# The last output tile: half of it copied out of PSUM by two engines and stored by rows on two queues

## The chip, the cores and the metric

The kernel runs on one core of one Trainium2 chip. The core has a matrix engine (PE in the profile), VectorE (DVE), ScalarE (ACT), GpSimd (POOL) and SyncE (SP), which work side by side and meet through semaphores, and 16 DMA engines that move data between the chip's main memory and the core. DMAs are issued here from two queues: SP's (SPq) and ScalarE's (ACTq). The metric is the device time of one execution in microseconds, from the start of the program to its end.

## The reference

The input `x` has 2048 rows of 512 bf16 numbers. It is normalised by rows, and two branches read the normalised rows: a linear attention with 32 heads and softmax feature maps, and a two-layer network of width 1792 with the mish activation. Both are added to `x`:

```python
x = A_x
xn = _layernorm(x, axis=-1)
return x + _A_ref(xn, A_wqkv, A_w_phi, A_wo) + _B_ref(xn, B_w1, B_b1, B_w2)
```

The attention ends in `o @ wo`, a product over 512 columns, and the network in `act @ w2`, a product over 1792. So one row of the output is the sum of three things: 14 products of 128 columns with `w2`, 4 with `wo`, and the row of `x` itself.

## The kernel before, in words

The 2048 rows are cut into 16 tiles of 128 rows. `x` lies in SBUF in one tile `x_sb` of 16 row tiles, is loaded at the start, and is overwritten by the output at the end. The weights lie in SBUF as well; `w2_sb` is loaded at about 20 us in three DMAs (line 646).

The order of all the work is written out by hand, as the names in `PLAN`; a loop at the end of the function calls `step` for each name, and each engine gets its instructions in that order. Nothing is moved by a scheduler. What the framework adds are the semaphores: each instruction waits for the writers and readers of the memory that it touches. The DMAs take their completion semaphores from a ring of eight, in the order in which they stand in the program, and a DMA waits for the DMA that had the same semaphore eight places before.

In the last stage, each output tile `t` goes through these names:

- `second_t_0` and `second_t_1` (`second_layer`, line 524): 14 matmuls of 128 rows and 512 columns from `acts` and `w2_sb` into one PSUM bank, `po`.
- `project_t` (`project_out`, line 533): 4 matmuls with `wo` into the same bank. Their input `ob` is a tile that a DMA on SP's queue transposed before (`turn_out`, line 512).
- `residual_t` (line 541): one VectorE instruction that adds `po` to the tile of `x_sb` and writes the tile back.
- `store_t` (line 545): a DMA of 128 rows of 1024 bytes to the output, on SP's queue.

The last tile, 15, is treated apart: `halves` gives it two halves of 256 columns, each with a PSUM bank of its own. So it has 28 + 8 matmuls of 256 columns, two additions on VectorE, and two stores of 128 rows of 512 bytes: that of the first half is issued on ScalarE's queue, that of the second on SP's. The end of the plan reads

```
project_12 second_15_0 residual_12 store_12 store_11 project_13 second_15_1 residual_13 store_13
project_14 project_15 residual_14 store_14 residual_15 store_15
```

After the last store the program waits for the semaphores of the DMAs that are still under way, and closes with two barriers over all engines.

Of the kernel before, what the change touches and what calls it, by code (L numbers as in the profile page):

```python
# [13 lines left out]
ALU = mybir.AluOpType  # L14
# [71 lines left out]
def kernel(  # L86
# [12 lines left out]
    nc = tc.nc  # L99
    P = 128  # L100
    S, D, NH, DH, F = 2048, 512, 32, 16, 1792
    NG = 4
    TPG = 4
    NT = NG * TPG
# [6 lines left out]
    o_v = out.flatten_outer_dims().rearrange("(t p) d -> p t d", p=P)  # L111
# [18 lines left out]
    def bank(name, dtype=FP32):  # L130
        return ps.tile([P, 512], dtype, name=name, tag="mm")

    x_sb = persist.tile([P, NT, D], BF16, name="x_sb")
# [15 lines left out]
    ident = consts.tile([P, P], BF16, name="ident")  # L149
# [46 lines left out]
    def spread(t):  # L196
        nc.vector.bn_stats(statistics(t)[0][:, t % TPG, :], x_sb[:, t, :])  # L197

    def total(t):
        negated.add(t)  # L200
        mv = statistics(t)[1][:, t % TPG, :]
        nc.scalar.activation(junk[:], x_sb[:, t, :], ACT.Identity, scale=-1.0 / D, accum_out=mv[:, 0:1])

    def scatter(t):
        mv = statistics(t)[1][:, t % TPG, :]
        nc.scalar.activation(
            junk[:], x_sb[:, t, :], ACT.Square, bias=mv[:, 0:1], accum_out=mv[:, 1:2]
        )

    def gather(t, n):  # L210
        stats, mv, _, _ = ln_of[t // TPG]
        for i in range(t % TPG, t % TPG + n):
            nc.vector.bn_aggr(mv[:, i, :], stats[:, i, :])

    def deviate(t, n):
        _, mv, rstd, _ = ln_of[t // TPG]
        i = slice(t % TPG, t % TPG + n)
        nc.scalar.activation(rstd[:, i], mv[:, i, 1], ACT.Sqrt, bias=eps[:],  # L218
            scale=1.0 / D if t in negated else 1.0)

    def invert(t, n):
        rstd = ln_of[t // TPG][2][:, t % TPG : t % TPG + n]
        nc.vector.reciprocal(rstd, rstd)  # L223
# [30 lines left out]
    def turn_pe(t):  # L254
        ptr = bank("ptr", BF16)
        for kt in range(KT):
            nc.tensor.transpose(  # L257
                ptr[:, kt * P : (kt + 1) * P], xn_of[0][:, t, kt * P : (kt + 1) * P], ident[:]
            )
        return ptr[:].rearrange("p (k c) -> p k c", k=KT)  # L260
# [255 lines left out]
    def halves(t):  # L516
        return (slice(0, 256), slice(256, 512)) if t == NT - 1 else (slice(0, 512),)

    def second_layer(t, f0, f1):
        if f0 == 0:  # L520
            po_of[t] = [bank("po") for c in halves(t)]
        for po, c in zip(po_of[t], halves(t)):
            for f in range(f0, f1):
                nc.tensor.matmul(  # L524
                    po[:, c], lhsT=acts[:, f, t * P : (t + 1) * P], rhs=w2_sb[:, f, c],
                    start=(f == 0), stop=False,
                )

    def project_out(t):
        h = t // 2  # L530
        for po, c in zip(po_of[t], halves(t)):
            for j in range(4):
                nc.tensor.matmul(  # L533
                    po[:, c], lhsT=oT_of[h][:, 2 + t % 2, j * P : (j + 1) * P], rhs=wo_sb[:, j, c],
                    start=False, stop=(j == 3),
                )

    def residual(t):
        for po, c in zip(po_of.pop(t), halves(t)):
            y = x_sb[:, t, c]  # L540
            nc.vector.tensor_tensor(out=y, in0=po[:, c], in1=y, op=ALU.add)  # L541

    def store(t):
        for n, c in enumerate(halves(t)):
            (nc.scalar if c.stop == 256 else nc.sync).dma_start(o_v[:, t, c], x_sb[:, t, c])


    with nc.allow_non_contiguous_dma(reason="tiny w_phi load"):
# [18 lines left out]
    for sign in (1, -1):  # L567
        nc.gpsimd.affine_select(
            out=block[:], in_=block[:], pattern=[[-16 * sign, 8], [0, 16]],
# [13 lines left out]
    def keep_warm():  # L583
        nc.tensor.matmul(warm[:], lhsT=one((P, P)), rhs=one((P, 512)), start=True, stop=True)
# [8 lines left out]
    def step(name):  # L593
# [5 lines left out]
        if kind == "warm":  # L599
            keep_warm()  # L600
        elif kind == "spread":
            spread(*n)
        elif kind == "block":
            nc.gpsimd.tensor_tensor(
                out=Wbd[:].rearrange("p j (h e) -> p j h e", h=8),
                in0=block[:, None, :, :].to_broadcast([P, 4, 8, 16]),
                in1=wsrc[:, :, None, :].to_broadcast([P, 4, 8, 16]),
                op=ALU.mult,
            )
        elif kind == "total":  # L610
            total(*n)
        elif kind == "scatter":
            scatter(*n)
        elif kind == "mean":
            gather(n[0], 1)
        elif kind == "deviate":
            deviate(*n)
        elif kind == "invert":
            invert(*n)
        elif kind == "flip":  # L620
            held[key] = turn_pe(*n)
        elif kind == "flip=":
            copies[alt](xnT[:, n[0], :, :], held.pop(key))  # L623
        elif kind == "foldk":
            held[key] = fold(held["wT"], *n)
        elif kind == "foldk=":
            copies[alt](wkp[:, n[0], :], held.pop(key)[:])  # L627
        elif kind == "first":
            i, kt = n
            held["logits", 0, i] = project(wkp, i, held.get(("logits", 0, i)), range(kt, kt + 1))  # L630
        elif kind == "bias":
            held[key] = bank("pb", BF16)
            nc.tensor.transpose(held[key][:, 0:FT], b1b[:], ident[0:FT, 0:FT])
        elif kind == "bias=":
            nc.vector.tensor_copy(b1f[:], held.pop(key)[:, 0:FT])
        elif kind == "gather":
            gather(TPG * n[0], TPG)
        elif kind == "root":
            root_inverse(*n)
        elif kind == "apply":  # L640
            apply(*n, sides[alt])
        elif kind == "turned":
            turn_dma(*n)
        elif kind == "w2":
            for f in (slice(0, 5), slice(5, 10), slice(10, 14)):
                nc.sync.dma_start(w2_sb[:, f, :], w2_v[:, f, :])
        elif kind == "wo":
            nc.sync.dma_start(wo_sb, wo_v[:, :, :])
        elif kind == "wq":
            held["wT"] = load_turned(0)  # L650
        elif kind == "fold":
            held[key] = fold(held["wT"], *n)
        elif kind == "fold=":
            copies[alt](wqp[:, n[0], :], held.pop(key)[:])
        elif kind == "value":
            held[key] = project(wv, *n)
        elif kind == "value=":
            value_copy(*n, held.pop(key), copies[alt])
        elif kind == "logits":
            held[key] = project(wkp if n[0] < NG else wqp, n[0] % NG * TPG + n[1])  # L660
        elif kind == "logits=" and n[0] in MERGED:
            signed_copy(*n, held[key], 1, sides[2 - 2 * alt])
        elif kind == "minus=":
            signed_copy(*n, held.pop(("logits", *n)), -1, sides[2 - 2 * alt])
        elif kind == "shift":
            shifted(n[0], slice(2 * n[1], 2 * n[1] + 2))
        elif kind == "logits=":
            logits_copy(*n, held.pop(key), copies[alt])
        elif kind == "plane":
            extremes(*n[0:2], *(slice(2 * q, 2 * q + 2) for q in n[2:]))  # L670
        elif kind == "exp":
            exponential(*n)
        elif kind == "sums":
            sums(*n, sides[alt])
        elif kind == "normal":
            normalise(*n)
        elif kind == "add":
            accumulate(*n)
        elif kind == "masks":
            masks()  # L680
        elif kind == "kv":
            mask_kv()
            kvp.close()
            later.append(ctx.enter_context(tc.tile_pool(name="pq", bufs=1, space=PSUM)))
        elif kind == "unit":
            held[key] = hidden(*n)
        elif kind == "unit=":
            activate(*n, held.pop(key))
        elif kind == "weigh":
            weigh(*n)  # L690
        elif kind == "turn":
            turn(*n)
        elif kind == "attend":
            attend(*n)
        elif kind == "divide":
            divide(*n)
        elif kind == "out":
            turn_out(*n)
        elif kind == "second":
            second_layer(n[0], 7 * n[1], 7 * n[1] + 7)  # L700
        elif kind == "project":
            project_out(*n)
        elif kind == "residual":
            residual(*n)
        elif kind == "store":
            store(*n)
# [33 lines left out]
```

## Time and profile before

| | |
|---|---|
| median of 3 runs | 174.26 us (174.21 to 174.62) |
| profiled execution | 174.22 us |
| its span, first to last instruction | 172.5 us |
| PE busy | 168.5 us, 98% of the span |
| VectorE busy | 150.6 us, 87% |
| ScalarE busy | 113.0 us, 66% |
| granted PE clock | 0.999 |

The profiled execution took 174.22 us, of which 172.5 us lie between its first and its last instruction; the 1.72 us that remain lie around the span. Times within the trace count from the start of the span. A row of the timeline gives the start and the length in microseconds, the engine, the line and the operation, what it writes and reads with the shape, how many instructions of a kind follow each other, and in brackets how long the engine had been idle before and what ended that. `SPq` and `ACTq` rows are the issuing of DMAs. A row of groups gives the total busy time and the mean duration of one in ns.

### The profile page before, as it was taken

How to read it: one execution, taken by the hardware profiler on the slowest of the kernel's cores; microseconds unless marked ns; L12 is line 12 of the kernel's file. 1: busy time of each engine (PE TensorE's matmuls, PEld its weight loads, DVE VectorE, ACT ScalarE, POOL GpSimd, SP SyncE). 2: the span in 40 equal slices, each digit the busy share in tenths (PEclk: the TensorE clock that was granted, in tenths of full speed). 3: DMA queues.
4: the chain of work that ended last, by engine and by line, in shares of the span. 5: the costliest groups of instructions: out<-in, count | busy, mean ns of one | idle time of the engine just before them, and what ended most of it. 6: DMA issues, size and time to landing. Idle time of an engine off the chain costs nothing.

```text
span 172.5 us, 2832 instructions
## 1 busy us (share of the span) xinstructions
PE 168.5 (98%) x1038; PEld 82.6 (48%) x1038; DVE 150.6 (87%) x265; ACT 113.0 (66%) x169; POOL 49.5 (29%) x91
## 2 busy tenths in 40 slices
PE   8999999999999999999999999999999999999993
PEld 2444444444544644455454444544544554445571
DVE  2967998999999999999999999999999899994633
ACT  4949999999999799999999998821710400400000
POOL 6003047100480005685007403341480420320000
PEclk9999999999999999999999999999999999999999
DMA  6999992647900000000000095217456556676752
GB/s 154 264 397 347 130 331 89 128 117 143 104 0 0 4 0 0 2 0 4 0 0 0 0 131 117 61 37 163 47 121 138 130 130 93 143 164 152 124 143 71
DMA packets 45226, 18.03 MB, mean 105 GB/s; under 512 B 37148, under 2 KB 45212, under 8 KB 45212
## 3 DMA queue, kind: packets, MB, share of 16 engines
q1 hardware_dynamic: 44496, 17.26, 44.5%
q10 hardware_dynamic: 716, 0.59, 1.1%
q8 instruction: 8, 0.13, 0.3%
q14 instruction: 6, 0.05, 0.1%
HBM read 6.84 MB, written 2.10 MB: 52 GB/s over the span
## 4 chain that ended last, share of the span: by engine, by line
PE 94%; DVE 2%; DMA 1%; ACT 1%; issue 0%; DVEq 0%
PE ph L289 28%; PE po L524 28%; PE pproj L274 24%; PE po L533 8%; PE pnd L488 2%; PE pkv L451 2%; DMA x_sb<-in_A_x_dram 1%; DVE stats L197 1%; PE pfold L174 1%; DVE x_sb L541 1%; PE ptr L257 1%; DVE xn L249 0%; ACT wkv L627 0%; ACT rstd L218 0%; DVE rstd L223 0%
## 5 line engine op out<-in xcount | busy, mean ns | idle before, releaser
L524 PE MATMUL po<-w_sb,acts 128*128 128x512 bf16 (+1 forms) x238 | 51.9, 366 | 0.0
L289 PE MATMUL ph<-xnT,w_sb 128*128 128x512 bf16 x224 | 50.9, 379 | 0.0
L377 ACT ACTIVATE e<-e 128x1024 bf16<-128x1024 bf16 x28 | 28.3, 1056 | 25.1 <-DVE e L347 25.0
L391 POOL TENSOR_TENSOR t<-e 128x512 f32<-128x512 bf16 x13 | 16.6, 1274 | 78.2 <-ACT e L377 78.1
L299 ACT ACTIVATE acts<-ph,b1f 128x512 bf16<-128x512 f32 x56 | 35.4, 706 | 1.2 <-PE ph L289 1.1
L289 PEld LDWEIGHTS <-w_sb 128*128 128x128 bf16 x224 | 21.5, 98 | 25.2 <-issue 0.4
L524 PEld LDWEIGHTS <-acts 128*128 128x128 bf16 x238 | 22.5, 98 | 22.9
L274 PE MATMUL pproj<-wkv,xnT 128*128 128x512 bf16 x128 | 29.4, 379 | 0.0
L274 PEld LDWEIGHTS <-xnT 128*128 128x128 bf16 x192 | 18.0, 98 | 20.1 <-ACT xnT L623 0.3
L387 DVE TENSOR_REDUCE sums<-e 128x64 f32<-128x1024 bf16 x15 | 17.9, 1212 | 1.0 <-ACT e L377 0.8
L391 POOL TENSOR_TENSOR t<-t 128x256 f32<-128x256 f32 (+1 forms) x28 | 16.1, 576 | 2.2
L533 PE MATMUL po<-wqk,ob 128*128 128x512 bf16 (+1 forms) x68 | 16.3, 366 | 0.0
L274 PE MATMUL pproj<-wqk,xnT 128*128 128x512 bf16 x64 | 15.3, 379 | 0.0
L541 DVE TENSOR_TENSOR x_sb<-po,x_sb 128x512 bf16<-128x512 f32 (+1 forms) x17 | 10.9, 650 | 4.1 <-PE po L533 4.1
L197 DVE BATCH_NORM_STATS2 stats<-x_sb 128x6 f32<-128x512 bf16 x15 | 9.4, 679 | 4.1 <-DMA x_sb<-in_A_x_dram 4.1
L504 DVE TENSOR_TENSOR ob<-pnd,r 128x512 bf16<-128x512 f32 x16 | 11.1, 691 | 0.5
L438 DVE TENSOR_TENSOR e<-e,r 128x2048 bf16<-128x2048 bf16 x8 | 9.9, 1231 | 0.3
L326 ACT CAST e<-pproj 128x512 bf16<-128x512 f32 x12 | 7.1, 605 | 4.4 <-PE pproj L274 3.9
L533 PEld LDWEIGHTS <-ob 128*128 128x128 bf16 x68 | 6.4, 98 | 6.0
L503 DVE RECIPROCAL r<-pnd 128x32 f32<-128x32 f32 x16 | 5.6, 351 | 4.0 <-PE pnd L488 3.8
L309 ACT CAST p<-pproj 128x512 bf16<-128x512 f32 x14 | 7.8, 597 | 1.6 <-PE pproj L274 1.6
L488 PEld LDWEIGHTS <-qT 128*128 128x128 bf16 x128 | 6.1, 97 | 3.9 <-issue 0.9
(80 smaller groups left out, 184.6 us busy)
## 6 DMA issues: line engine op xcount, KB each, us to landing
out_dram<-x_sb SPq DMA_DIRECT2D x15, 128.0 KB, 1.9
w_sb<-in_B_w_dram SPq DMA_DIRECT2D x2, 896.0 KB, 8.4
x_sb<-in_A_x_dram SPq DMA_DIRECT2D x3, 512.0 KB, 10.2
w_sb<-in_B_w_dram SPq DMA_DIRECT2D x2, 640.0 KB, 5.5
wkv<-in_A_wqkv_dram SPq DMA_DIRECT2D x1, 512.0 KB, 5.1
w_sb<-in_B_w_dram SPq DMA_DIRECT2D x1, 512.0 KB, 7.0
wqk<-in_A_wo_dram SPq DMA_DIRECT2D x1, 512.0 KB, 4.2
x_sb<-in_A_x_dram ACTq DMA_DIRECT2D x1, 384.0 KB, 3.2
```

What stands on the lines that cost most here:

```text
L197: nc.vector.bn_stats(statistics(t)[0][:, t % TPG, :], x_sb[:, t, :])
L274: nc.tensor.matmul(pp, lhsT=xnT[:, t, kt, :], rhs=w[:, kt, :], start=(kt == 0), stop=(kt == KT - 1),)
L289: nc.tensor.matmul(ph[:], lhsT=w1_sb[:, kt, f * P : (f + 1) * P], rhs=xnT[:, g * TPG : (g + 1) * TPG, kt, :], start=(kt == 0), stop=(kt == ...
L299: nc.scalar.activation(acts[:, f, g * 512 : (g + 1) * 512], ph[:], ACT.Mish, bias=b1f[:, f : f + 1])
L377: nc.scalar.activation(v, v, ACT.Exp)
L387: nc.vector.reduce_sum(out, part, axis=AX.X)
L391: nc.gpsimd.tensor_tensor(out=to[:], in0=part[:, :, 0:n], in1=part[:, :, n : 2 * n], op=ALU.add)
L438: nc.vector.tensor_tensor(out=vv, in0=vv, in1=r2[:, :, None, :].to_broadcast([P, 128, 8, 2]), op=ALU.mult)
L504: nc.vector.tensor_tensor(out=o_t.rearrange("p (u v g d) -> p u v g d", u=2, v=4, g=4), in0=nd[:, :, :, 0:64].rearrange("p u v (g d) -> p ...
L524: nc.tensor.matmul(po[:, c], lhsT=acts[:, f, t * P : (t + 1) * P], rhs=w2_sb[:, f, c], start=(f == 0), stop=False,)
L533: nc.tensor.matmul(po[:, c], lhsT=oT_of[h][:, 2 + t % 2, j * P : (j + 1) * P], rhs=wo_sb[:, j, c], start=False, stop=(j == 3),)
L541: nc.vector.tensor_tensor(out=y, in0=po[:, c], in1=y, op=ALU.add)
```

## The change

Three places are edited. In the last tile's second half (columns 256 to 511), an added matmul of the identity with the last 128 columns of `x` adds these columns into PSUM, right after the first matmul of that half. Its end is then written out in two parts: ScalarE copies columns 384 to 511, in which `x` is already contained, and VectorE adds columns 256 to 383 as before. The store of that half is cut by rows: rows 0 to 63 on ScalarE's queue, rows 64 to 127 on SP's. The store of the first half, which was on ScalarE's queue, is now issued on SP's. And `w2` is loaded in two DMAs of seven blocks in place of three of five, five and four, so that the number of DMAs in the program is as before.

```diff
@@ second_layer
                     start=(f == 0), stop=False,
                 )
+                if f == 0 and turned_in(t, c):
+                    nc.tensor.matmul(
+                        po[:, 384:512], lhsT=ident[:], rhs=x_sb[:, t, 384:512],
+                        start=False, stop=False,
+                    )
@@
+    def turned_in(t, c):
+        return t == NT - 1 and c.stop == D
+
     def residual(t):
         for po, c in zip(po_of.pop(t), halves(t)):
             y = x_sb[:, t, c]
-            nc.vector.tensor_tensor(out=y, in0=po[:, c], in1=y, op=ALU.add)
+            if turned_in(t, c):
+                nc.scalar.copy(out=y[:, 128:256], in_=po[:, 384:512])
+                nc.vector.tensor_tensor(
+                    out=y[:, 0:128], in0=po[:, 256:384], in1=y[:, 0:128], op=ALU.add
+                )
+            else:
+                nc.vector.tensor_tensor(out=y, in0=po[:, c], in1=y, op=ALU.add)
 
     def store(t):
         for n, c in enumerate(halves(t)):
-            (nc.scalar if c.stop == 256 else nc.sync).dma_start(o_v[:, t, c], x_sb[:, t, c])
+            if turned_in(t, c):
+                for q, rows in ((nc.scalar, slice(0, 64)), (nc.sync, slice(64, 128))):
+                    q.dma_start(o_v[rows, t, c], x_sb[rows, t, c])
+            else:
+                nc.sync.dma_start(o_v[:, t, c], x_sb[:, t, c])
@@ step
         elif kind == "w2":
-            for f in (slice(0, 5), slice(5, 10), slice(10, 14)):
+            for f in (slice(0, 7), slice(7, 14)):
                 nc.sync.dma_start(w2_sb[:, f, :], w2_v[:, f, :])
```

## The prediction

> **What bounds the kernel now.** I read the page's busy shares first, then the chain that ended last, then the timeline of the last four microseconds, engine by engine.
>
> ```profile
> span 172.5 us, 2832 instructions
> PE 168.5 (98%) x1038; PEld 82.6 (48%) x1038; DVE 150.6 (87%) x265; ACT 113.0 (66%) x169; POOL 49.5 (29%) x91
> ```
>
> PE is busy all the time; what follows its last matmul is uncovered. The chain, asked from 160 us on, shows both:
>
> ```profile
> 165.45 0.86 PE po L533 x4
> 166.31 1.53 PE po L524 x14
> 167.84 0.88 PE po L533 x4
> 168.72 0.02 issue
> 168.74 1.02 DVE x_sb L541 x2
> 169.76 0.33 DVEq L735
> ```
>
> PE's pieces follow each other without a gap, so whatever is added on PE there moves the end by its full length. From 168.74 the chain is VectorE's: tile 14's addition, then the two halves of tile 15. The timeline in short windows gives the pieces (a row that names several instructions runs from the first one's start to the last one's end):
>
> ```profile
> 168.74 0.69 DVE L541 TENSOR_TENSOR x_sb<-po,x_sb 128x512 bf16<-128x512 f32 x1 [1.70 <-PE po L533]
> 168.76 0.82 PE L533 MATMUL po<-wqk,ob 128*128 128x256 bf16 x6
> 169.68 0.41 DVE L541 TENSOR_TENSOR x_sb<-po,x_sb 128x256 bf16<-128x256 f32 x1
> 169.46 0.33 SPq L545 DMA_DIRECT2D out_dram<-x_sb  x1
> 169.79 0.37 ACTq L545 DMA_DIRECT2D out_dram<-x_sb  x1
> 170.12 0.33 SPq L545 DMA_DIRECT2D out_dram<-x_sb  x1
> ...
> out_dram<-x_sb ACTq DMA_DIRECT2D x1, 64.0 KB, 1.6
> out_dram<-x_sb SPq DMA_DIRECT2D x1, 64.0 KB, 1.5
> ```
>
> PE's last matmul ends at 168.76 + 0.82 = 169.58. VectorE's additions end at 169.43, 169.76 and 170.09, the third not waiting for PE but for VectorE. The three stores are issued 0.03 us after each addition, on SP, ACT and SP; SP's issue at 170.12 is over at 170.45 and lands 1.5 us after its start, at about 171.65, that is 1.2 us after its end. What follows, to 172.5, are the closing waits and barriers, the same in both kernels. So the kernel ends with SP's second-half store, and I count how far that landing moves.
>
> **The change, part by part.** *The identity matmul.* It moves 128 columns. PE has a run of that shape, 12 in a row, with the next matmul behind it:
>
> ```profile
> 59.54 0.83 PE L174 MATMUL pfold<-Wbd,wT 128*128 128x128 bf16 x12
> 60.21 0.38 PE L289 MATMUL ph<-xnT,w_sb 128*128 128x512 bf16 x1
> ```
>
> (60.21 − 59.54) / 12 = 0.056 us, weight loads included. It stands about 4.5 us before PE's end, in `second_15_0`, with nothing idle behind it on PE: **+0.06 us** on everything after. PE ends at 169.64, VectorE's two first additions at 169.49 and 169.82.
>
> *The two engines.* The aim is that ScalarE and VectorE read the half together. The built program has something else: VectorE's last instruction no longer waits for PE but for ScalarE's semaphore, at the value that the new copy gives it. It stands behind the copy, since both read the same bank `po`. The Trainium skill says why in *PSUM — Partial Sum Buffer*, section "PSUM bank collisions raise a hardware error": two engines may not touch one bank on the same partitions at once, two readers included, so their accesses are put one after the other. By that rule the half is ready at 170.26 (below) instead of 170.02; no run here shows a collision.
>
> The prices:
>
> ```profile
> L377 ACT ACTIVATE e<-e 128x1024 bf16<-128x1024 bf16 x28 | 28.3, 1056 | 25.1 <-DVE e L347 25.0
> L202 ACT ACTIVATE junk<-x_sb 128x512 bf16<-128x512 bf16 x1 | 0.6, 630 | 0.2 <-DMA x_sb<-in_A_x_dram 0.2
> L309 ACT CAST p<-pproj 128x512 bf16<-128x512 f32 x14 | 7.8, 597 | 1.6 <-PE pproj L274 1.6
> L564 ACT ACTIVATE root<-eps 128x1 f32<-128x1 f32 x1 | 0.2, 203 | 0.0
> L541 DVE TENSOR_TENSOR x_sb<-po,x_sb 128x512 bf16<-128x512 f32 x15 | 10.2, 682 | 4.1 <-PE po L533 4.1
> L541 DVE TENSOR_TENSOR x_sb<-po,x_sb 128x256 bf16<-128x256 f32 x2 | 0.7, 413 | 0.0
> ...
> 4.05 0.29 ACT L218 ACTIVATE rstd<-mv,eps 128x1 f32<-128x1 f32 x1
> 4.38 0.16 DVE L223 RECIPROCAL rstd<-rstd 128x1 f32<-128x1 f32 x1 [0.36 <-ACT rstd L218]
> ```
>
> ScalarE's slope is (1056 − 630) / 512 = 0.83 ns per column; the copy of 512 columns out of PSUM takes 597 ns, so 128 columns take 597 − 384 × 0.83 = 278 ns (between the 203 of one column and 597; I take 0.28). VectorE's slope is (682 − 413) / 256 = 1.05 ns, so 128 columns take 413 − 134 = 0.28 us (bounds: 0.41 for 256 columns, and 0.14 if there were no fixed part). From ScalarE's end to a VectorE start that waited for it, 4.34 to 4.38, are 0.04 us. So: PE ends 169.64; copy 169.67 to 169.95; VectorE 169.98 to 170.26. Before it was 170.09: this chain is **0.17 us later**, where side by side it would be 169.82 − 0.08 + 0.28 = 170.02 (the third addition of before started 0.08 before the second's end).
>
> *ScalarE's queue.* It issues rows 0 to 63 after VectorE: 170.29, +0.37. At 1.6 from issue to landing it would land at 171.89; the half-size store saves something (next part).
>
> *SP's queue.* It gets the first half's store between tile 14's and the last one: three issues on end where two stood 0.33 us apart. Issues that follow each other directly are longer than 0.33:
>
> ```profile
> 165.90 0.52 SPq L545 DMA_DIRECT2D out_dram<-x_sb  x1
> 166.46 0.94 SPq L545 DMA_DIRECT2D out_dram<-x_sb  x2
> ...
> 165.90 1.00 SPq L545 DMA_DIRECT2D out_dram<-x_sb  x2
> 164.53 1.26 SPq L512 DMA_TRANSPOSE ob<-ob  x1
> ...
> L545 SPq DMA_DIRECT2D out_dram<-x_sb x1: 430/430/430, 166.5 to 166.5; - x1
> L545 SPq DMA_DIRECT2D out_dram<-x_sb x1: 333/333/333, 167.1 to 167.1; - x1
> ```
>
> The first of these stores ends at 166.42, the second at 166.90: a period of 0.48 from end to end, with 0.43 for the issue itself. The third, begun after a pause, takes 0.33 again. In the changed kernel tile 14's store ends at 169.79 + 0.06 = 169.85. The first half's data is ready at 169.82, so its store ends at 169.85 + 0.48 = 170.33, and that of rows 64 to 127 at 170.81; its data, ready at 170.26, is not what it waits for. Before, the last issue ended at 170.45: **+0.36 us**. The bounds of a period: 0.43 (0.33 and a pause of 0.10, as between 165.79 and 165.90) gives 170.71, +0.26; the 0.63 behind a transpose (165.79 to 166.42) is a rival below.
>
> *The half-size store.* No row shows 64 rows. What is near:
>
> ```profile
> DMA to landing us min/median/max: 1.7/1.7/1.7
> ```
>
> That is the store of 128 KB at 167.07, with the same 0.33 issue as the 64 KB store at 1.5: half the bytes land 0.2 us sooner. Half the rows should save less, since half the bytes are left to save from: I take **−0.10 us**, bounds 0 and −0.2. SP's half then lands at 170.81 + 1.2 − 0.1 = 171.91, ScalarE's at 171.79.
>
> The Trainium skill, in *DMA: Bandwidth & Descriptors*, "Rules for kernel authors", speaks against such a split: two transfers for disjoint halves of the partitions share the same DMA engines and serialize, so one transfer of 128 partitions should be used. By it the −0.10 would be 0, and the sum 0.10 higher.
>
> *`w2` in two loads.*
>
> ```profile
> 19.74 1.75 SPq L646 DMA_DIRECT2D w_sb<-in_B_w_dram  x3
> 30.36 2.62 SPq L264 DMA_TRANSPOSE xnT<-xn  x2
> ...
> SPq L264 <- DVE sums L387: 9.9, 1, 9.9
> ```
>
> One issue of about 0.5 us goes. SP then idles for 8.9 us until VectorE releases the transpose, so it is worth nothing; the bytes are the same and are first read in the last stage. Were that cover gone, it would be a gain of 0.5 on SP alone. The ring of eight semaphores is as long as before at the end, and the waits there are for DMAs that landed long ago.
>
> **The sum.** +0.36 − 0.10 = +0.26 against 174.22, the profiled execution's own time: 174.48. The median of the three runs is 0.04 above that execution; I stay with 174.48. A measurement of this kernel can tell about 0.3% (0.52 us) from no change.
>
> **The rivals.**
>
> *A. Only the chain over ScalarE and VectorE decides.* SP's issues don't stack, and the later landing is ScalarE's, 171.79, or SP's with the short period, 171.81: +0.15, 174.37. For it: the 0.33 after a pause. Against it: every store issued within 0.06 us of another was longer.
>
> *B. The halves serialize on the DMA engines.* The rule just named, as a mechanism of this kernel: the −0.10 is missing, 174.58. For it: ScalarE's half starts 0.1 us before SP's, so they run together. Against it: fewer bytes landed sooner in the rows.
>
> *C. It works as meant:* the two engines do overlap, and SP's issues do not hold each other up. Ready at 170.02, issued to 170.38, landed at 171.48: −0.17, 174.05. Against it are the wait in the built program and the first half's store in SP's way.
>
> *D. Slower by more than 0.3%.* Place: SP's queue. Each of its two added periods is the 0.63 of a store behind another kind of DMA. The issue ends are 170.48 and 171.11, the landing is 172.21: +0.56, 174.78. It decides from a period of 0.62 on. For it: 0.52 is common for stores behind a transpose. Against it: here stores follow stores.
>
> **How the numbers follow.** The forecast, SP's queue at its 0.48 period, has 0.54; A 0.17; B 0.09; C 0.04; D 0.13; and 0.03 goes to a gain that no row shows. The forecast, A, B and C are within 0.3%: 0.84. D is slower: 0.13. Faster by over 0.3% is 0.03, for the whole stretch from PE's end to the landing is 2.1 us, and no part names 0.5 of it. The range 174.2 to 174.8 takes in the forecast, A and B with the bounds 0 and −0.2 of the half-size store, and reaches up to D.
>
> **What would show it.** In the changed kernel's profile: a row of one identity matmul, and PE's end 0.06 later; VectorE's 128-column addition starting only after the ScalarE copy's end, at about 170.0; three SP issues on end behind 169.5, the second and third longer than 0.33, the last ending near 170.8; landing of the 64-row stores near 1.4 us from issue. Wrong would be the forecast if VectorE's last addition began before the copy ended, if the last SP issue ended before 170.5, or if a 64-row store needed as long as one of 128 rows or far less. Beyond all this, a stretch before 165 us that moved would show an effect that I hold to be nil.

## The result, and the profile after

The changed kernel takes 175.29 us (median of 5 runs, 175.21 to 175.63), the kernel before 174.26 (174.21 to 174.62, 5 runs): the ratio is 1.0057, 95% interval 1.0044 to 1.0070. So it is about 1.0 us slower, where 0.26 us was forecast and 174.8 was the upper end of the range. The profiled execution took 175.48 us, with a span of 173.7.

First the chain that ended last in the changed kernel, from 166 us on (start, length, engine, what is written, line):

```profile
168.40 1.75 PE po L538 x12
170.15 0.02 issue
170.18 0.28 ACT x_sb L550
170.45 0.02 issue
170.47 0.29 DVE x_sb L551
```

Before, VectorE's three additions on end closed this chain; now the end of PE's work, the ScalarE copy and one addition follow each other. The two engines do not work side by side. Then the rows of the timeline that follow PE's last matmul, and the stores' sizes and median times to landing:

```profile
169.76 0.38 PE L538 MATMUL po<-wqk,ob 128*128 128x256 bf16 x2
170.02 0.33 SPq L563 DMA_DIRECT2D out_dram<-x_sb  x1
170.45 0.38 SPq L563 DMA_DIRECT2D out_dram<-x_sb  x1
170.80 0.54 ACTq L561 DMA_DIRECT2D out_dram<-x_sb  x1
170.92 0.56 SPq L561 DMA_DIRECT2D out_dram<-x_sb  x1
...
out_dram<-x_sb ACTq DMA_DIRECT2D x1, 32.0 KB, 1.8
out_dram<-x_sb SPq DMA_DIRECT2D x1, 32.0 KB, 2.0
```

PE ends at 170.14. The data of the last half is complete at 170.47 + 0.29 = 170.76, which is 0.62 us after PE's end; before it was 0.51 (169.58 to 170.09). SP's last issue begins 0.16 us after that (before 0.03) and is the longest of the four: 0.56 us for half as many rows as the last store of the kernel before, which took 0.33. It lands 2.0 us after its start; that whole store took 1.5. From PE's end to the end of the span that makes 173.7 − 170.14 = 3.6 us against 172.5 − 169.58 = 2.9: 0.67 us more, of which 0.11 is the two engines, 0.13 SP's queue, and 0.44 the last store itself (in the events behind these rows, 1.98 us against 1.54). From the last landing to the end of the span it is 0.83 us against 0.84, so what closes the program did not change.

The packets that the DMA engines moved show where the 0.44 lies. In the kernel before, the first packet of SP's last store moves 0.84 us after the issue begins, in the changed kernel 1.34; from the first packet to the last it is 0.36 us before and 0.30 now; from the last packet to the landing 0.34 both times. So moving half the rows does take 0.06 us less, but it begins 0.50 us later. ScalarE's packets (queue q10) and SP's (q1) come one after the other. These are the packets, megabytes and share of two windows, from 171.7 to 172.26 us, where SP's queue moves nothing, and from 172.3 to 172.6, where ScalarE's moves nothing:

```profile
q10 hardware_dynamic: 79, 0.03, 23.3%
...
q1 hardware_dynamic: 73, 0.03, 39.5%
```

PE's own end is 0.56 us later. The identity matmul accounts for 0.06 of it:

```profile
165.14 0.22 PE L529 MATMUL po<-x_sb,ident 128*128 128x128 bf16 x1
165.19 0.82 PE L524 MATMUL po<-w_sb,acts 128*128 128x256 bf16 x6
```

The next matmul starts 0.05 to 0.06 us behind it, as priced. The other 0.5 us comes from the start, in code that the change does not touch. The first transposes begin 0.63 us later, and 0.13 of it is made up on the way:

```profile
6.21 0.29 PE L257 MATMUL ptr<-ident,xn 128*128 128x128 bf16 x2 [0.52 <-DVE xn L249]
```

The same transposes began at 5.58 in the kernel before:

```profile
5.58 0.40 PE L257 MATMUL ptr<-ident,xn 128*128 128x128 bf16 x4 [0.16 <-DVE xn L249]
```

In the changed kernel VectorE waited longer for a load of `x`:

```profile
5.14 0.69 DVE L197 BATCH_NORM_STATS2 stats<-x_sb 128x6 f32<-128x512 bf16 x1 [0.54 <-DMA x_sb<-in_A_x_dram]
```

In the kernel before, it did not wait before this instruction. This start differs from execution to execution of both kernels (5.6 to 6.2 us in the profiles below, whatever was changed), so I compare stretches that begin at PE's end, and the medians.

### The profile page after: what moved, and what is told of

The parts are those of the page before. It is cut to its first block, busy times and chain, and to the rows that moved or that the text cites. A ratio compares the mean times of both kernels' runs of the same rounds, so it can differ in the third digit from the quotient of the medians.

```text
span 173.7 us, 2820 instructions
## 1 busy us (share of the span) xinstructions
PE 167.7 (96%) x1022; PEld 82.7 (48%) x1039; DVE 150.7 (87%) x265; ACT 113.4 (65%) x170; POOL 49.5 (28%) x91
## 4 chain that ended last, share of the span: by engine, by line
PE 88%; DVE 6%; DMA 2%; issue 1%; ACTq 0%; ACT 0%; DVEq 0%
PE ph L289 28%; PE po L524 24%; PE pproj L274 23%; PE po L538 7%; PE pkv L451 2%; DMA x_sb<-in_A_x_dram 2%; PE pnd L488 2%; DVE ob L504 1%; DVE m L340 1%; DVE stats L197 1%; DVE e L347 1%; DVE x_sb L555 1%; DVE sums L387 1%; PE ptr L257 1%; PE pfold L174 1%
## 5 line engine op out<-in xcount | busy, mean ns | idle before, releaser
L524 PE MATMUL po<-w_sb,acts 128*128 128x512 bf16 (+1 forms) x232 | 51.2, 366 | 0.4
```

The lines of the kernel that those rows point to most:

```text
L524: nc.tensor.matmul(po[:, c], lhsT=acts[:, f, t * P : (t + 1) * P], rhs=w2_sb[:, f, c], start=(f == 0), stop=False,)
```

## The experiments

**1. `w2` alone.** The kernel before with `for f in (slice(0, 7), slice(7, 14))`.

> The kernel before with w2 loaded in two DMAs and nothing else changed. Of the 1.0 us by which the changed kernel is slower, its trace puts 0.06 on the identity matmul, 0.11 on the copy and the addition behind it, and about 0.56 on the last stores, between VectorE's last addition and the last landing; the rest lies ahead of the first matmuls, where the first loads of x landed about 0.6 us later. Theory T (the start only varies from run to run): 174.2 to 174.4, as before. Rival W (the new program loads later, because of the w2 edit): 174.5 to 174.7, with PE's first transposes near 6.2 us instead of 5.6.

Measured: 174.35 us against 174.35, ratio 1.0004 (0.9993 to 1.0016), PE's first transposes at 5.67 us. So Theory T holds and not Rival W. The loads of `w2` are worth nothing, as predicted, and the late start does not come with them.

**2. The stores alone.** The computation of before, the changed kernel's `store` and `w2`.

```diff
-            (nc.scalar if c.stop == 256 else nc.sync).dma_start(o_v[:, t, c], x_sb[:, t, c])
+            if turned_in(t, c):
+                for q, rows in ((nc.scalar, slice(0, 64)), (nc.sync, slice(64, 128))):
+                    q.dma_start(o_v[rows, t, c], x_sb[rows, t, c])
+            else:
+                nc.sync.dma_start(o_v[:, t, c], x_sb[:, t, c])
```

> The kernel before, with the changed kernel's stores (first half on SP, second half by rows on ScalarE's queue and SP's) and its two w2 loads; no identity matmul, no ScalarE copy: VectorE adds both halves as before. If the stores cost what the trace after says, about 174.8 (+0.5 to +0.6), with both 64-row issues at 0.5 us or more in place of 0.33 to 0.37. If the stores only follow the late data in the changed kernel (rival: the copy and its wait are the cause), 174.3 to 174.4.

Measured: 175.02 us against 174.35, ratio 1.0041 (1.0026 to 1.0055): +0.7 us without any of the new computation, a little over the expected +0.5 to +0.6. Its timeline:

```profile
170.45 0.53 ACTq L550 DMA_DIRECT2D out_dram<-x_sb  x1
170.69 0.56 SPq L550 DMA_DIRECT2D out_dram<-x_sb  x1
```

The issues are as long as in the changed kernel. The stores are the main loss.

**3. The same by columns.** The kernel of experiment 2 with 128 rows of 128 columns on each queue.

```diff
-                for q, rows in ((nc.scalar, slice(0, 64)), (nc.sync, slice(64, 128))):
-                    q.dma_start(o_v[rows, t, c], x_sb[rows, t, c])
+                for q, cols in ((nc.scalar, slice(256, 384)), (nc.sync, slice(384, 512))):
+                    q.dma_start(o_v[:, t, cols], x_sb[:, t, cols])
```

> As the kernel with the row stores alone, but the second half is cut by columns: 128 rows of 256 bytes on each of the two queues, issued at the same moment. Theory R (64 rows are what makes an issue long): the issues take 0.33 to 0.40 us, and the kernel about 174.3 to 174.5. Theory C (two queues that issue at the same moment hold each other up): the issues take 0.5 us or more, and the kernel about 174.8, as with rows.

Measured: 174.59 us against 174.35, ratio 1.0013 (1.0000 to 1.0026), over the expected 174.3 to 174.5.

```profile
170.83 0.37 ACTq L550 DMA_DIRECT2D out_dram<-x_sb  x1
171.07 0.40 SPq L550 DMA_DIRECT2D out_dram<-x_sb  x1
...
out_dram<-x_sb ACTq DMA_DIRECT2D x1, 32.0 KB, 1.5
out_dram<-x_sb SPq DMA_DIRECT2D x1, 32.0 KB, 1.5
```

The same number of stores, the same bytes each, the two issues overlapping in the same way, and they are short and land after 1.5 us. So two queues that issue together do not explain the 0.54 and 0.56; the cut by rows does. The 0.24 us that are left go with the third store in SP's queue: its issue begins 0.27 us after VectorE has completed the data, at 170.80, and not 0.03 as before.

**4. The matmul, the copy and the addition alone.** The changed kernel with `store` and the `w2` loads of before.

> The changed kernel's matmul, copy and addition, with the stores and the w2 loads of the kernel before (first half on ScalarE's queue, second half whole on SP's). If the copy and the addition stand one after the other as the program's wait says: +0.06 on PE, +0.11 after it, so about 174.4 to 174.5. If the two-engine part were the main loss: 174.8 or more.

Measured: 174.54 us against 174.35, ratio 1.0011 (1.0000 to 1.0021): +0.2 us, as the two terms +0.06 and +0.11 say, just over the expected 174.4 to 174.5. With the 0.7 us of experiment 2 it makes 0.9; the whole change measured 1.0 above and 0.9 in experiment 12. The rows stand as in the changed kernel, the addition right behind the copy:

```profile
169.60 0.27 ACT L550 CAST x_sb<-po 128x128 bf16<-128x128 f32 x1 [19.46 <-PE po L538]
...
169.90 0.29 DVE L551 TENSOR_TENSOR x_sb<-po,x_sb 128x128 bf16<-128x128 f32 x1
```

**5. Both half-row stores on SP.** The changed kernel, with `nc.sync` for both row halves and the first half's store back on ScalarE's queue.

> The changed kernel with both half-row stores on SP's queue, one behind the other, and the first half's store back on ScalarE's queue. Theory R (64 rows are what makes an issue long, whatever the other queue does): both issues take 0.5 us or more though no other queue issues beside the second of them; the second ends 0.25 us later than in the changed kernel, so 175.2 to 175.5. Theory C (the two queues hold each other up): 0.33 and 0.43 us, 174.5 to 174.7.

Measured: 175.71 us against 174.38, ratio 1.0074 (1.0058 to 1.0089), a little over the expected 175.2 to 175.5.

```profile
169.85 0.37 ACTq L563 DMA_DIRECT2D out_dram<-x_sb  x1
169.97 0.29 DVE L551 TENSOR_TENSOR x_sb<-po,x_sb 128x128 bf16<-128x128 f32 x1
170.29 1.19 SPq L561 DMA_DIRECT2D out_dram<-x_sb  x2
...
out_dram<-x_sb SPq DMA_DIRECT2D x2, 32.0 KB, 1.9
```

No other queue issues between 170.29 and 171.48, and the two stores of 64 rows still take 1.19 us. Concurrent issuing is excluded a second time as what makes them long. They land 1.84 and 1.88 us after their start, so about 0.3 us more than a whole store needs is there without a second store of 64 rows beside them; in the changed kernel SP's store needed 0.10 more than that.

**6. A bank of its own for ScalarE's part.** The kernel of experiment 4 with three banks for the last tile:

```diff
-        return (slice(0, 256), slice(256, 512)) if t == NT - 1 else (slice(0, 512),)
+        return (slice(0, 256), slice(256, 384), slice(384, 512)) if t == NT - 1 else (slice(0, 512),)
...
-                nc.scalar.copy(out=y[:, 128:256], in_=po[:, 384:512])
-                nc.vector.tensor_tensor(
-                    out=y[:, 0:128], in0=po[:, 256:384], in1=y[:, 0:128], op=ALU.add
-                )
+                nc.scalar.copy(out=y, in_=po[:, c])
```

> As the changed kernel's matmul, copy and addition with the stores of the kernel before, but columns 384 to 511 have a PSUM bank of their own, so that ScalarE's copy and VectorE's last addition read different banks; the last half's matmuls become twice as many of 128 columns. If the shared bank is what puts the addition behind the copy: the addition starts before the copy ends or at its end, without waiting for it, about 0.1 us after PE's end, and the second half is complete about 0.1 us sooner after PE's end than with one bank; PE ends up to 0.05 later. In all 174.3 to 174.5. If another thing puts it behind the copy, the addition still starts 0.03 after the copy.

Measured: 174.45 us against 174.38, ratio 1.0005 (0.9994 to 1.0016).

```profile
169.46 0.61 DVE L552 TENSOR_TENSOR x_sb<-po,x_sb 128x256 bf16<-128x256 f32 x2
169.74 0.27 ACT L550 CAST x_sb<-po 128x128 bf16<-128x128 f32 x1 [19.50 <-PE po L538]
```

VectorE's two additions now end at 170.07 and overlap the copy, which runs from 169.74 to 170.01. The data is complete 0.33 us after the copy's start, with one bank 0.59 (169.60 to 170.19). So sharing is what put the addition behind the copy. The edit gives ScalarE's part a bank of its own and with it a tile of its own, so this run doesn't tell which of the two it is. The interval overlaps that of experiment 4 (1.0000 to 1.0021), so a gain in the whole is not shown.

**7, 10, 11. How the number of rows counts.** The kernel before, with the stores of tiles 8 to 14 on ScalarE's queue, which has no other work by then, cut by rows:

```diff
+    cuts = {8: (48, 80), 10: (128,), 9: (112, 16), 12: (32, 96), 11: (128,), 13: (64, 64), 14: (16, 112)}
+            r = 0
+            for n in cuts[t]:
+                nc.scalar.dma_start(o_v[r : r + n, t, :], x_sb[r : r + n, t, :])
+                r += n
```

These lines are those of experiment 10; 7 and 11 have other numbers.

> The kernel before, with the stores of tiles 8 to 13 on ScalarE's idle queue, cut by rows: 64+64, 32+96, 128, 16+112, 128, 96+32. Theory R1 (any store of fewer than 128 rows is issued in a slower way): the first issue of each cut store takes about 0.5 us or more, that of a whole one 0.37. Theory R2 (the cost falls as rows are added): 16 rows longest, 96 and 112 near 0.4. Theory R3 (only concurrency with SP counts): all near 0.37 unless SP issues at the same time.

> The kernel before, with the stores of tiles 8 to 14 on ScalarE's queue, cut by rows: 48+80, 112+16, 32+96, 64+64, 16+112, two whole. Theory S: from a pause, 32 and 16 rows take about 0.33 to 0.38 us, 64 rows 0.53 or more. Rival B (what counts is a power of two under 128): 32 and 16 rows take 0.5 or more from a pause as well, and only 96, 112, 80 and 48 are short.

> As the run before with other cuts: 96+32, 64+64, 48+80, 32+64+32, 80+48. Theory S: the 64 rows that begin at row 32 take 0.53 or more too, 48 and 80 rows 0.33 to 0.44. Rival P (the place counts: rows that begin at 0 or 64): the 64 rows from row 32 take 0.43 to 0.48, like any issue behind another.

From a pause, 96 rows took 0.32 us in experiment 7 and the first 64 rows 0.54, while 16 rows behind another issue took 0.44. So neither R1 nor R2 held. R3 was left open, since SP issued a store at the same moment as the 64 rows (150.77 and 150.78 us). Experiment 10 settles it: no SP issue stands between 165.04 and 170.69 us. Its rows, first tile 12, then both halves of 13, then 14 (the size tells the rows, 1 KB each; last the median time to landing):

```profile
165.25 0.32 ACTq L549 DMA_DIRECT2D out_dram<-x_sb  x1
...
out_dram<-x_sb ACTq DMA_DIRECT2D x1, 32.0 KB, 1.5
...
167.64 0.54 ACTq L549 DMA_DIRECT2D out_dram<-x_sb  x1
...
out_dram<-x_sb ACTq DMA_DIRECT2D x1, 64.0 KB, 2.0
...
168.22 0.60 ACTq L549 DMA_DIRECT2D out_dram<-x_sb  x1
...
out_dram<-x_sb ACTq DMA_DIRECT2D x1, 64.0 KB, 2.1
...
170.03 0.33 ACTq L549 DMA_DIRECT2D out_dram<-x_sb  x1
...
out_dram<-x_sb ACTq DMA_DIRECT2D x1, 16.0 KB, 1.4
```

32 rows 0.32, 64 rows 0.54, 64 rows 0.60, 16 rows 0.33. In experiment 11, 48 rows from a pause took 0.33, 80 rows 0.32, and the 64 rows that begin at row 32 took

```profile
L549 ACTq DMA_DIRECT2D out_dram<-x_sb x1: 567/567/567, 167.6 to 167.6; - x1
```

behind another issue, where 16, 32, 48, 80, 96, 112 and 128 rows behind another issue took 0.43 to 0.44. An issue that followed one of 64 rows was long too (32 rows, 0.59). So of the counts tried, 64 alone is slow, at row 0, 32 and 64, on both queues; what is special about it the runs don't show. Left out are issues beside SP's transposes between 158 and 160 us, which were long with other counts too (16 rows up to 0.65, 112 rows 0.62, 96 rows 0.56; 64 rows up to 0.67). The single times of these three kernels (174.98, 175.54 and 174.90 us) say nothing on the question.

**8. A version meant to beat both.** The kernel before, with the last tile cut into 384 and 128 columns, and the first part finished before the second begins:

```diff
-        return (slice(0, 256), slice(256, 512)) if t == NT - 1 else (slice(0, 512),)
+        return (slice(0, 384), slice(384, 512)) if t == NT - 1 else (slice(0, 512),)
...
-project_12 second_15_0 residual_12 store_12 store_11 project_13 second_15_1 residual_13 store_13
-project_14 project_15 residual_14 store_14 residual_15 store_15
+project_12 second_15_0 residual_12 store_12 store_11 project_13 residual_13 store_13
+project_14 second_15_1 project_15 residual_14 store_14 residual_15 store_15
...
+        if t == NT - 1:
+            if f0:
+                project_part(t, 0)
+            second_part(t, 1 if f0 else 0, 0, FT)
```

> A version meant to beat both: the kernel before with its last tile cut into 384 and 128 columns, the 384 finished first (second layer and projection), then the 18 matmuls of the last 128 columns, which are PE work of about 1.0 us beside VectorE's other additions. No ScalarE copy, no identity, whole stores. VectorE's last addition is then of 128 columns (0.28 us instead of 0.41) and waits for PE instead of for VectorE: the last data is ready 0.32 to 0.36 us after PE's end instead of 0.52, PE ends up to 0.05 later; so 174.1 to 174.2, 0.1 to 0.2 us under the kernel before. If the store of 256-byte rows lands later, or PE loses more to the smaller matmuls, no gain.

Measured: 174.06 us against 174.38, ratio 0.9977 (0.9966 to 0.9988): 0.3 us faster than the kernel before, where 0.1 to 0.2 was expected, and with it faster than the changed kernel. Its timeline:

```profile
169.35 0.39 PE L541 MATMUL po<-wqk,ob 128*128 128x128 bf16 x4
169.36 0.37 ACTq L556 DMA_DIRECT2D out_dram<-x_sb  x1
169.77 0.29 DVE L552 TENSOR_TENSOR x_sb<-po,x_sb 128x128 bf16<-128x128 f32 x1 [0.45 <-PE po L541]
...
out_dram<-x_sb SPq DMA_DIRECT2D x1, 32.0 KB, 1.5
```

VectorE sits idle for 0.45 us until PE has ended, at 169.74, and the data is complete at 170.06: 0.32 us after PE's end, before 0.51. A store of 256-byte rows lands no later than one of 512-byte rows (1.46 us against 1.54). From PE's end to the end of the span that makes 2.65 us against 2.93.

**9. The changed kernel with the rows cut at 96.**

```diff
-                for q, rows in ((nc.scalar, slice(0, 64)), (nc.sync, slice(64, 128))):
+                for q, rows in ((nc.scalar, slice(0, 96)), (nc.sync, slice(96, 128))):
```

> The changed kernel with one number changed: the second half's store is cut into rows 0 to 95 on ScalarE's queue and rows 96 to 127 on SP's. The stores of other counts than 64 that ran before took no longer than whole ones (96 rows 0.32 us from a pause; 16, 32 and 112 rows 0.43 to 0.44 behind another issue), those of 64 rows 0.53 to 0.58. Theory S (64 rows alone are slow): issues of 0.37 and about 0.38 to 0.43, and the kernel at 174.6 to 174.9, 0.4 to 0.6 us under the changed one. Rival H (any store cut by rows that stands at the end of the kernel is slow): 0.5 us or more again, 175.2 to 175.4.

Measured: 174.74 us against 174.54, ratio 1.0014 (1.0004 to 1.0024), as Theory S expected.

```profile
170.25 0.34 ACTq L561 DMA_DIRECT2D out_dram<-x_sb  x1
170.37 0.40 SPq L561 DMA_DIRECT2D out_dram<-x_sb  x1
...
out_dram<-x_sb ACTq DMA_DIRECT2D x1, 48.0 KB, 1.6
out_dram<-x_sb SPq DMA_DIRECT2D x1, 16.0 KB, 1.6
```

One number, and most of the loss is gone: the ratio falls from 1.0057 (1.0049 in the repetition below) to 1.0014. By this ratio the kernel costs 0.24 us, near the forecast's 0.26, but not by the forecast's terms: its small stores land 1.60 and 1.65 us after their start, no sooner than the whole ones of before with 1.62 and 1.54, so the saving of 0.10 isn't there either. Here the packets of the two queues do overlap. In the window from 171.28 to 171.49 us both move:

```profile
q1 hardware_dynamic: 46, 0.02, 29.6%
q10 hardware_dynamic: 43, 0.02, 30.8%
```

**12. The changed kernel again.**

> The changed kernel as it is, once more. From PE's last matmul to the end, its first profile is 0.67 us longer than that of the kernel before, and the identity matmul adds 0.06, together 0.73, while the medians lie 1.03 apart. If the other 0.3 is the start, which varies from run to run (PE's first transposes began at 5.6 to 6.2 us in the profiles so far), the ratio here is about 1.004, and the stretch from PE's end to the end of the span again 3.5 to 3.6 us. If it is a part of the change that the stretch does not show, the ratio is again 1.005 to 1.007 with a start near 5.6.

Measured: 175.23 us against 174.36, ratio 1.0049 (1.0030 to 1.0069), the stretch behind PE's end 3.6 us again.

```profile
170.76 0.56 SPq L561 DMA_DIRECT2D out_dram<-x_sb  x1
```

The start was early this time, 5.64 us, but PE's end was at 169.97, 0.39 later than in the kernel before and only 0.06 of it by the identity matmul. From PE's first transposes to its end it took 164.33 us here, 164.00 in the kernel before, 163.93 in the first profile of the changed kernel, and 164.30 in experiment 3, which has no identity matmul: this stretch differs from execution to execution too. 0.73 of 174.36 is 0.0042, inside this interval and just under the first one's 0.0044. The early start and the ratio fit the second reading of the expectation, and the interval holds the first one too. Whether the 0.1 to 0.3 us by which the medians lie further apart are chance ahead of the last stage or belong to the change is not settled.

## Why the prediction was wrong, point by point

The step that failed is **the half-size store**: −0.10 us with the bounds 0 and −0.2. Measured, the store of 64 rows needs 0.44 us more from the start of its issue to its landing than the whole one, not 0.10 less. In its own terms, the sum counted up to the end of the last issue and from there to the landing. Behind PE's end the first was to grow by 0.30 us and grew by 0.46; the second was to shrink by 0.10, from 1.2 to 1.1, and grew by 0.21, to 1.42. Together that is 0.20 forecast and 0.67 measured. I had two rows of 128-row stores with different bytes and extended them to fewer rows, and I took the issue to be as long for any count. The idea that fewer bytes move faster was right, with 0.06 us; that the first packet would come 0.50 us later had no term. The prediction had named a 64-row store that needs as long as one of 128 rows as a sign that it was wrong; it needed longer. Other counts bear the saving out only in part: with rows of 1024 bytes, 32 rows landed after 1.5 us and whole ones after 1.7, but in experiment 9 the smaller stores landed no sooner. The bound from the nearest rows was no bound, since no row had 64 rows in it.

**SP's queue**, +0.36, was right in its mechanism and its size up to the last issue: the second issue's end came 0.48 us after the first's (170.35 to 170.83), the period that I took. The third period was 0.65 instead of 0.48, since the third issue is one of 64 rows; these 0.17 us are the miss up to the last issue's end. Rival D had a period of that size, but for another reason and in both places.

**The two engines.** The wait in the built program was read rightly. The copy took 0.27 us (0.28 priced), the addition 0.29 (0.28), the data was complete 0.11 us later behind PE's end (0.17 less the 0.06 of the identity). The Trainium skill's rule on PSUM banks, *PSUM — Partial Sum Buffer*, "PSUM bank collisions raise a hardware error", agrees with experiments 4 and 6 as far as they go: with a bank of its own the copy overlaps the addition, with the shared bank the addition follows it by 0.03 us. What would happen without the wait no run shows.

**The identity matmul**, +0.06, and **`w2`**, nothing, were right.

**The rivals.** B, the rule that disjoint halves of the partitions serialize, was the only one that put the store's saving at nothing. Its advice, one store of 128 partitions, holds here. Its reason explains at most a small part: the 64-row stores of experiment 5, one behind the other on one queue, land about 0.3 us later than whole ones, and the packets of the cut into 96 and 32 rows overlap. In the changed kernel, where SP's issue begins 0.12 us behind ScalarE's, SP's packets begin only as ScalarE's end, and its store takes 1.98 us, 0.10 more than those of experiment 5; in experiment 2, where it begins 0.23 behind, it takes 1.89. Whether these 0.10 us are the two halves serializing is not tested. Why the first packet of a 64-row store comes late stays open. A and C are excluded by the rows: the addition began after the copy, and SP's issues followed each other with periods of 0.48 and 0.65. D's place was right and its sign too.

**The chances.** I gave 0.13 to a loss over 0.3%. What should have widened the range upwards is that a shape of DMA that no row of the trace shows stood last on the path, with nothing behind which it could hide.

## What to carry to other kernels

A DMA whose shape the trace has never shown has no upper bound from its neighbours; at the end of a kernel, where its whole length is exposed, a single look at it is worth more than an estimate, and here 64 rows cost 0.2 us more to issue than 128 and, the issue included, 0.44 more to land. ScalarE and VectorE read the last tile side by side only when each had its own bank; read the waits of the built program before crediting the overlap. To shorten a tail, look for the engine that is behind PE at the end and give it less to do last: finishing 384 columns early and leaving 128 gained what the split over engines and queues did not.

## What was not expected of the hardware

- A store of 64 rows takes 0.53 to 0.58 us to issue and 1.8 to 2.0 us to land when rows have 512 bytes; whole ones 0.33 to 0.38 and 1.5 to 1.6. Away from transposes, stores of 16, 32, 48, 80, 96 and 112 rows are issued no more slowly than whole ones (0.32 to 0.35 from a pause, 0.40 to 0.44 behind another issue). With 64 rows of 1024 bytes the issue takes 0.54 from a pause as well, so it is the count and not the length of a row.
- The issue that follows one of 64 rows 0.04 us later is long too, in the one case with other than 64 rows: 0.59 for 32 rows, against 0.44 behind any other count.
- Two queues that issue ordinary stores at the same time lengthen each other's issues little (0.37 and 0.40 us in experiment 3; at most, 0.40 for 96 rows in experiment 11, 0.04 us apart from an SP store, against 0.32 alone).
- Issues that follow each other at once, away from transposes, keep a period of 0.48 us from end to end (0.50 in experiments 3 and 9, where the other queue issues beside them), whatever the number of rows but 64.
